# Four attention blocks forward and backward on one core: the queue of the last drain in a written order, and the weight-gradient operands in swapped buffers

## The chip, the cores and the metric

The kernel runs on one core of one Trainium2 chip. The core has a matrix engine (TensorE, PE in the profile; its weight loads are the rows PEld), a vector engine (VectorE, DVE), a scalar engine (ScalarE, ACT), a general engine (GpSimd, POOL) and a sync engine (SyncE, SP) that here only issues DMA transfers. The metric is the device time of one execution in microseconds (us); lower is better.

## The reference

Two kinds of block, A and B, follow each other as A, B, A, B on an input of 2048 rows by 640 columns, with 32 heads of width 20. The second A uses the weights of the first, and the second B those of the first B. The reference returns the output and the gradients of the input and of the four weight matrices.

```
def _A_ref(x, wqkv, wo):                 # linear attention
    q, k, v = split(x @ wqkv)
    phi = lambda t: where(t > 0, t + 1, exp(t)) + 1e-6
    pq, pk = phi(q), phi(k)
    kv, z = einsum("bhsd,bhse->bhde", pk, v), einsum("bhsd->bhd", pk)
    o = einsum("bhqd,bhde->bhqe", pq, kv) / (einsum("bhqd,bhd->bhq", pq, z) + 1e-6)
    return o @ wo
def _B_ref(x, wqkv, wo):                 # attention to the last 256 rows
    p = softmax(where(mask, q @ k.T * Dh ** -0.5, -1e9))
    return (p @ v) @ wo
x = A_x
x = x + _A_ref(_layernorm(x), A_wqkv, A_wo)
x = x + _B_ref(_layernorm(x), B_wqkv, B_wo)
x = x + _A_ref(_layernorm(x), A_wqkv, A_wo)
x = x + _B_ref(_layernorm(x), B_wqkv, B_wo)
out, vjp = jax.vjp(f, A_x, A_wqkv, A_wo, B_wqkv, B_wo); grads = vjp(grad_out)
```

All arrays are bfloat16. The blocks are called layers 0 to 3 below: 0 and 2 are A, 1 and 3 are B.

## The kernel before, in words

The rows are cut into 16 tiles of 128. `passes` is a generator that runs the whole program in stages: the forward pass of all layers, the backward core of layer 3, the backward pass of layer 2, the backward core of layer 1, and then, without a break, the last drain, the backward pass of layer 0 and the weight gradients. `run` asks for one stage after the other. For each it opens a block in which the order of the instructions on an engine is the order in which Python emits them. PE, DVE, ACT and POOL are always in that block. SP is in it only where the entry of `SPM` is true; elsewhere the framework's scheduler chooses the place of each DMA issue in SP's queue. SP works through its queue strictly in order: an issue that has to wait holds up every later one.

Two other devices set the order. `slots` spreads a list of small functions over numbered slots, by the offsets in the table `PLACES`. And where SP is in order, `put` doesn't issue a DMA at once: it stores it with a delay in slots from `PLACES["sp"]`, and `tick`, called once a slot, issues what is due.

**The core of a B layer** goes over eight chunks of two tiles. What follows a chunk (`plan_behind`) turns its gradient `dq` (128 x 2 x 1920) into `dqT`, multiplies with `WTB` into `dh`, closes the layer norm (`lna`, `gn`), turns `gn` (`gT`), multiplies with `WoTA` into `dn`, and adds an outer product of `dn` and `pqb` into `macc`. It loads `hnb`, `gc`, `oa` and `pqb`, and stores `dq`, `gn` and `dn`. For the last two chunks, 6 and 7, most of that happens after the core has ended.

**The last drain** is that rest for layer 1: a list `left1` of functions, one a slot. It is also where the weight gradients begin, since their matmuls need nothing from the drain. `weight_jobs` is a generator of them: a job is one block of columns of one weight matrix, five groups of 32 matmuls (128 x 160 for Wo of B, 128 x 240 for W of B, then wider ones for A). A group needs `lhs`, two halves of four DMAs each (640 KB a DMA), and `rhs`, four DMAs of 320 KB for Wo of B. Matmuls 0 to 15 of a group read the first half of `lhs`, 16 to 31 the second; each DMA feeds four of them. After a group, DVE or ACT copies the sum into `wr`, which has five buffers and is stored by one DMA. `fill(us)` takes matmuls from the generator up to a credit of so many us.

At slot 8 of the drain the generator is called for the first time, which issues all loads of the first job. From slot 25 on, each slot emits its own function and then `fill(1.0)`. After the drain `macc` is closed into `dmz` and turned.

**The backward pass of layer 0** follows with 16 tiles of eight slots each, with `fill(0.8)` a slot. A tile loads `ldn`, `lv`, `lpqk`, `lhn`, `lg` for two tiles at a time, turns three of them on PE (L205), forms `dqa`, turns it, multiplies with `WTA` and stores `dqa` to DRAM (`dqkv`). `dqa` has two buffers. When the last job of Wo of B ends, the second half of the next `lhs` is loaded into a buffer that this job has used. The generator then asks for 8.0 us of credit without any matmul, so ten slots pass that hold no weight-gradient matmul; this is called the gap below. When the layer is finished, the remaining weight gradients run alone.

**Buffers.** The first job's `lhs` halves (the stored `o` of layers 3 and 1) come from one pool `wl` of two buffers, first buffer first. The first of these lies where the last `dq` of the core was.

Lines: `put` L134, `tick` L142, the drain L1520 to L1561, the store of a weight-gradient block L1299. All DMA issues have line L129, nearly all matmuls L185 and the turns of PE L205, L1082, L1158 and L252.

Of the kernel before, what the change touches and what calls it, by code (L numbers as in the profile page):

```python
# [15 lines left out]
P = 128  # L16
# [5 lines left out]
TT = T // P  # L22
DT = D // P
SPM = (True, True, False, True, False)
G = H // 4
# [24 lines left out]
    sp=[4, 2.1, 1, 0.6, 2.6, -2.1, 0.5, 0.4, 2, 1.8, 1.1, 0.8, 3, 1, 0.9, 0.5, 1.3, 1.1, 1, 1],  # L50
# [3 lines left out]
    bl3=[13.4, 15, 15.5, 16.2, 17.3, 17.7, 18.5, 20.2, 25.9, 28.6, 29.3, 36, 19.7, 19.9, 20.3, 22.7, 23.9, 24.8, 26.3, 26.7, 30.1, 31.8, 33.1, 36.4, 40.2, 44.6, 13.4, -5.7, -4.4, 14, 19.4, 35.1],  # L54
    bl1=[13.4, 15, 15.8, 16.8, 17.4, 17.7, 19.7, 21.4, 26.1, 27.8, 30.5, 36, 19.2, 20, 20.3, 21.7, 23.7, 24.6, 25.1, 25.9, 29.6, 31.8, 32.8, 35.8, 40.1, 44.6, 0, -6, -5, -2, 0, 1],
    la=[-10.3, -2.5, 2.1, 2.4, 1.9, 3.2, 4.6, 6.2, 7.2, 8, 4.9, 8, 8.3, 10, 11.8, 13.9, 14, 16.2, 16.9, 17, 19.2, -2.3, 3.6],
# [13 lines left out]
    xx=[1, 0, 1, 1, 0, 0, 0, 0, 1, 0, 1, 0, 0, 0, 0, 0, 0, 1, 0, 0, 1, 0, 0, 1],  # L70
    bd=[0, 1, 0, 0, 0, 0, 0, 1, 0, 1, 1, 0, 1, 1, 0, 0, 0, 1, 1, 1, 0, 1, 0, 0])


class Kern:
# [58 lines left out]

    def put(self, kind, out, in_, transpose=False, now=False):  # L134

        d = PLACES["sp"][kind]
        if not self.spm or d <= 0 or now:
            self.dma(out, in_, transpose)
        else:
            self.queue.append((self.now + d, len(self.queue), out, in_, transpose))  # L140
# [804 lines left out]
    def plan_behind(self, st, l, c, dq, g_out):  # L945

        nc = self.nc
        la = l - 1
        x = {}
        r = self.r[la]  # L950
        last = c == TT // 2 - 1
        ex = last and l == 1

        def load():
# [3 lines left out]
        def turn(i):  # L958
            assert dq["n", c] == 8
            x["dT", i] = st.sp.tile([P, NF, P], BF, name="dqT", bufs=3)  # L960
            if c == TT // 2 - 2 or (c == TT // 2 - 1 and i == 0):
                self.turn_pe(st, x["dT", i], dq[c][:, i, :])
            else:
                self.put(7, x["dT", i], dq[c][:, i, :], transpose=True)

        def store():
            assert dq["n", c] == 8
            self.put(8, self.pair(self.dq[l], c), dq.pop(c))

# [6 lines left out]
        def store_g():  # L976
            assert x["gn", 0] and x["gn", 1]
            self.put(9, self.pair(g_out, c), x["gn"])

        def store_dn():  # L980
            assert x["rd", 0] is not None and x["rd", 1] is not None
            self.put(10, self.pair(self.sv[la]["dn"], c), x["dn"].rearrange("p b h d -> p b (h d)"))

# [235 lines left out]
    def weight_jobs(self, W):  # L1219
# [54 lines left out]
        while job is not None:  # L1274
# [6 lines left out]
            for m in range(DT):  # L1281
                if m == 1:
                    job = after(i0, c0, w)
                    if job is not None:
                        nxt = ls, rhs(mats[job[0]][1], job[1], job[2])
                if m == 2 and job is not None and job[1] == 0:
                    L2 = mats[job[0]][0]
                    nxt = [lhs(L2[0]), None if W.tight else lhs(L2[1])], nxt[1]
                ps = W.ps.tile([P, 512], F32, name="wg")
                for i in range(n):  # L1290
                    self.mm(ps[:, 0:w], ls[i // TT][:, i % TT, m * P:(m + 1) * P], r[:, i, 0:w], i == 0, i == n - 1)
                    if i < n - 1:
                        yield w / 2400.0
                o = W.out()
                if m % 2:
                    nc.scalar.copy(o[:, 0:w], ps[:, 0:w])  # L1296
                else:
                    nc.vector.tensor_copy(o[:, 0:w], ps[:, 0:w])  # L1298
                self.dma(out[m * P:(m + 1) * P, c0:c0 + w], o[:, 0:w])  # L1299
                yield w / 2400.0  # L1300
# [136 lines left out]
    def passes(self):  # L1437
# [6 lines left out]
        with ExitStack() as rest:  # L1444
# [80 lines left out]
            W.ps = self.pool(rest, "wp", 2, bass.MemoryType.PSUM, "right")  # L1525
            wl = self.pool(rest, "wl", 2)
            W.big, W.turn, W.wide, W.late = self.pool(rest, "wq", 1).tile([P, 2, 2 * TT, 240], BF, name="rhs"), 0, False, None
            wo = self.pool(rest, "wo", 5)
            st.ex = self.pool(psl, "ex", 1)
            W.lhs, W.tight = [wl, wl], True  # L1530
            W.out = lambda: wo.tile([P, 240], BF, name="wr")
# [10 lines left out]
            for j, f in enumerate(left1):  # L1542
                if f is not None:
                    f()
                if j == 8:
                    next(jobs)
                if j == 20:
                    self.fetch(WTA, self.WT["A"])
                if j > 24:
                    fill(1.0)  # L1550
            self.close_outer(self.dmz)
            self.turn_outer(st, self.dmz, self.dmzT)
            psl.close()
            es.close()

            with ExitStack() as es, ExitStack() as le:
# [15 lines left out]
            wl4 = self.pool(rest, "wl", 2)  # L1572
            W.lhs += [wl4, wl4, wl, wl3]
            W.tight, W.wide = False, True
# [70 lines left out]
```

## Time and profile before

| | |
|---|---|
| time, median of 3 runs | 2173.22 us (2174.26, 2164.63, 2173.22) |
| the profiled execution | 2163.42 us, span 2161.7 us |
| PE busy | 2021.7 us, 94% of the span |
| DVE / ACT / POOL busy | 65% / 61% / 48% |
| DMA on SP's queue | 674976 packets, 420.52 MB |

The span is the time from the first to the last instruction of the profiled execution, and its own time is 1.7 us longer. The profile gives, for each engine, the busy time in windows; for a group of instructions, its count, its mean duration and what ended the idle time before it; for SP, when each DMA was issued and how long until it landed; and a chain of waits followed back from the last instruction. A row of the timeline holds a start, a duration, and the number of instructions of one kind that followed each other without a break; the duration of a run of matmuls contains the passage of the last one through the array. In the profile the drain begins at about 1648 us, the first turn of layer 0's backward pass (`flip<-ident,ldn`) is at 1729.17 us, its last matmul is at 1945.8 us, and the rest is weight gradients.

### The profile page before, as it was taken

Reading aid. Unit: us, or ns where it says so; the run is one execution under the profiler, and the core shown is the slowest. Engines: PE = TensorE matmul, PEld = TensorE weight load, DVE = VectorE, ACT = ScalarE, POOL = GpSimd, SP = SyncE. Lnnn points to the kernel's source line nnn. Section 1 sums busy time; section 2 is a strip of 40 time slices with the busy share of each in tenths; the row PEclk is TensorE's granted clock in tenths of the full one; section 3 lists DMA queues with packets and bytes.
Section 4 is the critical chain, followed back from the end, with each engine's and each line's share of the span. In section 5 each row is a group of like instructions: output and inputs, shape, how many; then the busy total and the mean of one; then the engine's idle time right before and its main releaser. Section 6 shows DMA issues by size and latency. Waiting matters only on the chain.

```text
span 2161.7 us, 77047 instructions
## 1 busy us (share of the span) xinstructions
PE 2021.7 (94%) x32885; PEld 1563.7 (72%) x32885; DVE 1400.5 (65%) x2828; ACT 1314.6 (61%) x1866; POOL 1032.9 (48%) x1643
## 2 busy tenths in 40 slices
PE   8889998899987999999979999999998899999999
PEld 6667776677766877777758778777776788888644
DVE  7789996788844888888748678888885233320000
ACT  6568887478875787777647667777775143330000
POOL 1046666156666577777524566777764111220000
PEclk9999999999999999999999999999998999999999
DMA  7598886698874379898899724899987899978650
GB/s 250 198 233 209 213 213 168 199 226 217 216 200 139 92 157 191 188 191 179 182 283 274 199 75 122 185 188 188 191 182 194 264 306 229 285 193 263 204 164 21
DMA packets 675320, 425.45 MB, mean 197 GB/s; under 512 B 399264, under 2 KB 653984, under 8 KB 674592
## 3 DMA queue, kind: packets, MB, share of 16 engines
q1 hardware_dynamic: 674976, 420.52, 76.3%
q8 instruction: 257, 4.21, 0.8%
q14 instruction: 87, 0.71, 0.1%
HBM read 195.17 MB, written 144.70 MB: 157 GB/s over the span
## 4 chain that ended last, share of the span: by engine, by line
PE 49%; DVE 8%; POOL 7%; DMA 6%; ACT 5%; issue 4%; SPq 1%; DVEq 0%; POOLq 0%; ACTq 0%
PE dense L185 16%; PE wg L185 15%; DVE ds L790 5%; PE acc L185 4%; PE dp L185 3%; PE flip L205 3%; PE flip L812 2%; POOL e L805 2%; DMA pqb<-pqk 1%; ACT e L786 1%; PE sT L185 1%; PE ops L185 1%; PE flip L216 1%; POOL e L801 1%; SPq L129 1%
## 5 line engine op out<-in xcount | busy, mean ns | idle before, releaser
L790 DVE TENSOR_TENSOR ds<-dp,e 128x1024 bf16<-128x1024 f32 (+1 forms) x384 | 443.7, 1155 | 120.8 <-PE s L185 70.6
L786 ACT ACTIVATE e<-s 128x1024 bf16<-128x1024 f32 (+1 forms) x384 | 374.9, 976 | 113.0 <-PE s L185 91.4
L448 ACT ACTIVATE eT<-sT 128x2048 bf16<-128x2048 f32 x180 | 338.0, 1878 | 94.1 <-PE sT L185 64.7
L185 PE MATMUL wg<-rhs,lhs 128*128 128x240 bf16 (+3 forms) x2880 | 373.7, 286 | 9.7 <-DMA lhs<-o 9.7
L185 PEld LDWEIGHTS <-lhs 128*128 128x128 bf16 x2880 | 260.7, 98 | 99.4 <-DMA lhs<-o 12.5
L805 POOL TENSOR_SCALAR_AFFINE_SELECT e<-e 128x256 bf16<-128x256 bf16 x512 | 207.5, 421 | 164.4 <-ACT e L786 164.1
L185 PEld LDWEIGHTS <-dqT 128*128 128x128 bf16 x1920 | 174.4, 98 | 60.0 <-issue 4.4
L456 POOL TENSOR_SCALAR_AFFINE_SELECT eT<-eT 128x512 bf16<-128x512 bf16 x256 | 165.2, 649 | 104.5 <-ACT eT L448 101.3
L185 PE MATMUL acc<-slabqs,ds 128*128 128x20 bf16 x2880 | 195.6, 172 | 2.1 <-ACT dq L874 0.4
L185 PE MATMUL acc<-ds,e 128*128 128x20 bf16 x2880 | 193.3, 171 | 0.0
L185 PEld LDWEIGHTS <-ds 128*128 128x128 bf16 x2880 | 173.2, 96 | 19.7 <-issue 15.3
L185 PE MATMUL dp<-slabT,dT 32*128 32x128 bf16 (+1 forms) x1952 | 150.0, 244 | 29.4 <-DVE ds L790 23.4
L1298 DVE CAST wr<-wg 128x240 bf16<-128x240 f32 (+3 forms) x54 | 24.4, 452 | 233.0 <-PE wg L185 228.1
L801 POOL TENSOR_SCALAR_AFFINE_SELECT e<-e 128x512 bf16<-128x512 bf16 x224 | 142.5, 636 | 59.6 <-ACT e L786 55.1
L185 PEld LDWEIGHTS <-e 128*128 128x128 bf16 x2880 | 164.2, 96 | 5.0 <-issue 0.9
L1296 ACT CAST wr<-wg 128x240 bf16<-128x240 f32 (+3 forms) x36 | 14.3, 396 | 245.8 <-PE wg L185 233.2
L1190 POOL TENSOR_TENSOR dh<-dh,lg 128x640 f32<-128x640 f32 x32 | 46.1, 1440 | 242.7 <-DVE s L1187 240.2
L185 PE MATMUL dense<-WB,hnT 128*128 128x320 bf16 x960 | 160.0, 303 | 1.7 <-ACT hnT L208 0.7
L185 PE MATMUL dense<-WTA,dqT 128*128 128x320 bf16 x960 | 158.0, 301 | 0.6 <-DVE dqT L1161 0.3
L812 PE MATMUL flip<-ident,ds 128*128 128x128 bf16 x1920 | 152.9, 221 | 3.4 <-DVE ds L911 3.4
L185 PE MATMUL dense<-WTB,dqT 128*128 128x320 bf16 x960 | 153.8, 301 | 0.0
L185 PE MATMUL s<-slabT,slabqT 32*128 32x128 bf16 (+1 forms) x1952 | 147.0, 245 | 4.5 <-ACT e L786 4.5
(184 smaller groups left out, 4478.4 us busy)
## 6 DMA issues: line engine op xcount, KB each, us to landing
T<-T SPq DMA_DIRECT2D x96, 256.0 KB, 4.1
s<-s SPq DMA_DIRECT2D x32, 512.0 KB, 3.1
slabT<-T SPq DMA_DIRECT2D x64, 256.0 KB, 3.6
dqkv<-dq SPq DMA_DIRECT2D x16, 960.0 KB, 6.9
dqkv<-dqa SPq DMA_DIRECT2D x32, 480.0 KB, 4.3
rhs<-dqkv SPq DMA_DIRECT2D x32, 480.0 KB, 5.7
rhs<-dqkv SPq DMA_DIRECT2D x16, 960.0 KB, 7.7
hn<-hn SPq DMA_DIRECT2D x64, 160.0 KB, 3.5
```

The source lines that it names most:

```text
L129: return self.nc.sync.dma_start(out=out, in_=in_, transpose=transpose)
L185: return self.nc.tensor.matmul(out, lhsT=lhsT, rhs=rhs, start=start, stop=stop, skip_group_check=True, **kw)
L205: self.nc.tensor.transpose(t[0:w, j, :], src[:, c0:c0 + w], self.ident)
L448: nc.scalar.activation(e, s, ACT.Exp)
L456: nc.gpsimd.affine_select(out=e, in_=e, compare_op=ALU.is_ge, fill=0.0, base=0, pattern=[[0, 4], [1, P]], channel_multiplier=-1)
L786: nc.scalar.activation(u.e[:, :, 0:w], s[:, :, 0:w], ACT.Exp)
L790: nc.vector.tensor_tensor(out=d.ds[:, :, 0:w], in0=d.dp[:, :, 0:w], in1=d.e[:, :, 0:w], op=ALU.mult)
L801: nc.gpsimd.affine_select(out=v, in_=v, pattern=[[0, 4], [1 if far else -1, P]], **kw)
L805: nc.gpsimd.affine_select(out=v, in_=v, pattern=[[0, 2], [1 if far else -1, P]], **kw)
L812: nc.tensor.transpose(ps[:, 4 * j + i, :], f.ds[:, j, i * P:(i + 1) * P], self.ident)
L1190: nc.gpsimd.tensor_tensor(out=x["dh"], in0=x["dh"], in1=L["g"][:, i, :], op=ALU.add)
L1298: nc.vector.tensor_copy(o[:, 0:w], ps[:, 0:w])
```

## The change

Four things are changed. `SPM` gets a sixth entry and `passes` one more `yield`, so that the last drain is a stage of its own with SP in Python's order, and layer 0's backward pass starts a new stage in which the scheduler places the DMA issues as before. In the drain, DMAs that go through `put` get delays from the new table `sd` for the last two chunks: the `dq` store has none, the stores of `gn` and `dn` wait about three slots, the store of a weight-gradient block 3.5 slots (`dj`). The first job's loads are issued after slot 3 and not 8, and a slot's credit is 0.7 and not 1.0, so fewer weight-gradient matmuls stand in the drain and more behind it. The last chunk's offsets `bl1` are slightly different. And the two `lhs` buffers are two pools of one buffer, taken in the other order.

```diff
-SPM = (True, True, False, True, False)
+SPM = (True, True, False, True, True, False)
...
-    bl1=[13.4, 15, 15.8, 16.8, 17.4, 17.7, 19.7, 21.4, 26.1, 27.8, 30.5, 36, 19.2, 20, 20.3, 21.7, 23.7, 24.6, 25.1, 25.9, 29.6, 31.8, 32.8, 35.8, 40.1, 44.6, 0, -6, -5, -2, 0, 1],
+    bl1=[12.9, 15.1, 15.5, 16.2, 18.1, 19.6, 20.2, 22.2, 25.7, 27.8, 30.7, 34.2, 18.7, 19.4, 21.1, 21.6, 23.4, 24.3, 24.3, 25.9, 29.6, 31, 33.3, 35.3, 40.9, 45, 0.5, -4.8, -3.6, -1.2, 0.5, 1],
...
+    sd=[0.7, 0, 0, 3, 3, 3, 3, 3.9, 0, 0, 3.2, 2.6, 3.3, 3.1],
+    dj=[3, 21.9, 24, 3.5, 0.7, 8])
...
-    def put(self, kind, out, in_, transpose=False, now=False):
+    def put(self, kind, out, in_, transpose=False, now=False, delay=None):
-        d = PLACES["sp"][kind]
+        d = PLACES["sp"][kind] if delay is None else delay
...
+        tail = max(c - TT // 2 + 3, 0)
+        def wait(n):
+            return PLACES["sd"][n + 7 * (l == 1)] if tail else None
...
-                self.put(7, x["dT", i], dq[c][:, i, :], transpose=True)
+                self.put(7, x["dT", i], dq[c][:, i, :], transpose=True, delay=wait(0) if last else None)
...
-            self.put(8, self.pair(self.dq[l], c), dq.pop(c))
+            self.put(8, self.pair(self.dq[l], c), dq.pop(c), delay=wait(tail))
...
-            self.put(9, self.pair(g_out, c), x["gn"])
+            self.put(9, self.pair(g_out, c), x["gn"], delay=wait(2 * tail + 1))
...
-            self.put(10, self.pair(self.sv[la]["dn"], c), x["dn"].rearrange("p b h d -> p b (h d)"))
+            self.put(10, self.pair(self.sv[la]["dn"], c), x["dn"].rearrange("p b h d -> p b (h d)"), delay=wait(2 * tail + 2))
...
-                self.dma(out[m * P:(m + 1) * P, c0:c0 + w], o[:, 0:w])
+                self.put(0, out[m * P:(m + 1) * P, c0:c0 + w], o[:, 0:w], delay=PLACES["dj"][3])
...
-            wl = self.pool(rest, "wl", 2)
+            wl, wl2 = self.pool(rest, "wl", 1), self.pool(rest, "wl", 1)
...
-            W.lhs, W.tight = [wl, wl], True
+            W.lhs, W.tight = [wl2, wl], True
...
-                if j == 8:
+                if j == min(int(PLACES["dj"][0]), len(left1) - 2):
                     next(jobs)
-                if j == 20:
+                if j == min(int(PLACES["dj"][1]), len(left1) - 1):
                     self.fetch(WTA, self.WT["A"])
-                if j > 24:
-                    fill(1.0)
+                if j > PLACES["dj"][2]:
+                    fill(PLACES["dj"][4])
+                self.tick()
             self.close_outer(self.dmz)
             self.turn_outer(st, self.dmz, self.dmzT)
+            self.flush()
             psl.close()
             es.close()
+            yield
...
-            W.lhs += [wl4, wl4, wl, wl3]
+            W.lhs += [wl4, wl4, wl2, wl3]
```

What this makes of the order, engine by engine: up to the first transfers of the drain nothing moves. POOL's order is the same throughout, DVE and ACT exchange neighbours in the drain. On PE the same matmuls stand in another mixture: 236 weight-gradient matmuls ahead of the turn of `dmz` instead of 316, and 376 instead of 460 ahead of the first turn of `ldn`. The gap falls one tile later: before, it holds the turns of tile 2's and tile 3's `ldn`, after the change those of tile 3's and tile 4's. On SP the order in the drain is new, and behind it the scheduler puts the loads and stores of layer 0 and of the weight gradients in other places too:

```
before: hnb, gc, oa, pqb, rhs x4, dqT(chunk 7), dqkv(6), oa, pqb, dqkv(7), g, rhs, lhs x8, WTA, dn, wr1, rhs x3, wr2, g ...
after:  hnb, dqkv(6), oa, gc, oa, pqb(6), dqkv(7), dqT(7), pqb(7), rhs, lhs x2, rhs, lhs x2, rhs, lhs x2, rhs, lhs x2, g, WTA, rhs x4, dn, wr1, wr2, g ...
```

In the last part the eight `lhs` loads of Wo of A stand, before, one after the 56th and seven after the 57th stored block, with two `rhs` loads after the 55th. After the change one stands behind the 54th, two behind the 56th and five behind the 57th, and their `rhs` loads behind the 52nd to the 55th. That job starts when 60 blocks are done.

More of the change, by code (lines that the diff above doesn't have):

```diff
@@ L70 @@
     xx=[1, 0, 1, 1, 0, 0, 0, 0, 1, 0, 1, 0, 0, 0, 0, 0, 0, 1, 0, 0, 1, 0, 0, 1],
-    bd=[0, 1, 0, 0, 0, 0, 0, 1, 0, 1, 1, 0, 1, 1, 0, 0, 0, 1, 1, 1, 0, 1, 0, 0])
+    bd=[0, 1, 0, 0, 0, 0, 0, 1, 0, 1, 1, 0, 1, 1, 0, 0, 0, 1, 1, 1, 0, 1, 0, 0],
+    sd=[0.7, 0, 0, 3, 3, 3, 3, 3.9, 0, 0, 3.2, 2.6, 3.3, 3.1],
+    dj=[3, 21.9, 24, 3.5, 0.7, 8])
 class Kern:
```

## The prediction

> **What bounds the kernel now.** I read the page first, then the waits of PE from the drain on, then PE's and SP's timelines where those waits lie, and last the windows. From the page:
>
> ```profile
> span 2161.7 us, 77047 instructions
> PE 2021.7 (94%) x32885; PEld 1563.7 (72%) x32885; DVE 1400.5 (65%) x2828; ACT 1314.6 (61%) x1866; POOL 1032.9 (48%) x1643
> PE 49%; DVE 8%; POOL 7%; DMA 6%; ACT 5%; issue 4%; SPq 1%; DVEq 0%; POOLq 0%; ACTq 0%
> ```
>
> PE bounds it, and the change adds no matmul and removes none. It can move the time only through PE's idle time and through matmuls at the lower clock. SP's order differs from 1648 us on, PE's from about 1672. PE's waits from 1655 us to the end:
>
> ```profile
> PE wg L185 <- DMA lhs<-o: 9.7, 9, 1.7
> PE flip L1082 <- DVE dqa L1131: 4.1, 1, 4.1
> PE flip L205 <- POOL gn L1040: 1.9, 2, 1.2
> ```
>
> Columns are total us, times, longest. Some 16 us are in play. Six of the nine `lhs` waits lie in the drain; here they are in PE's timeline, with what follows:
>
> ```profile
> 1681.62 0.72 PE L185 MATMUL wg<-rhs,lhs 128*128 128x160 bf16 x8
> 1683.23 0.45 PE L185 MATMUL wg<-rhs,lhs 128*128 128x160 bf16 x4 [0.89 <-DMA lhs<-o]
> ...
> 1690.44 0.71 PE L185 MATMUL wg<-rhs,lhs 128*128 128x160 bf16 x4 [1.09 <-DMA lhs<-o]
> 1692.20 0.58 PE L185 MATMUL wg<-rhs,lhs 128*128 128x160 bf16 x3 [1.05 <-DMA lhs<-o]
> ...
> 1693.11 2.21 PE L185 MATMUL wg<-rhs,lhs 128*128 128x160 bf16 x15
> ...
> 1696.31 1.20 PE L185 MATMUL wg<-rhs,lhs 128*128 128x160 bf16 x15
> ```
>
> PE takes four matmuls from each `lhs` DMA as it lands. The six waits end 1.79 us apart, which for 0.655 MB is 366 GB/s. Fifteen matmuls then take 2.21 us, later 1.20. Why so late, in SP's timeline:
>
> ```profile
> 1649.95 1.43 SPq L129 DMA_DIRECT2D rhs<-in_grad_out_dram  x2
> 1651.42 4.21 SPq L129 DMA_DIRECT2D rhs<-g  x2
> 1661.56 1.66 SPq L129 DMA_TRANSPOSE dqT<-dq  x1
> ...
> 1666.54 0.58 SPq L129 DMA_DIRECT2D dqkv<-dq  x1
> ...
> 1673.80 9.31 SPq L129 DMA_DIRECT2D lhs<-o  x8
> 1683.15 2.27 SPq L129 DMA_DIRECT2D WTA<-WTAt  x1
> ```
>
> The first `lhs` DMA is issued 7.26 us after the second `dqkv` store. That store takes 6.5 us to land (median of two), and the first `lhs` buffer lies over the `dq` it reads. The windows (length, busy us of PE, PEld, DVE, ACT, POOL, clock, DMA share, GB/s):
>
> ```profile
> 1650.00:1660.00 10.00, 8.83 (x63) 7.12 (x63) 2.76 (x5) 2.53 (x5) 0.00 (x0) 0.57 0.94 249
> 1680.00:1690.00 10.00, 4.67 (x41) 3.09 (x39) 2.23 (x6) 2.39 (x5) 4.47 (x3) 0.80 1.08 374
> 1690.00:1700.00 10.00, 8.51 (x88) 7.70 (x89) 1.37 (x3) 1.68 (x3) 0.00 (x0) 0.69 0.97 346
> 1800.00:1850.00 50.00, 50.00 (x530) 44.37 (x528) 15.56 (x41) 18.18 (x38) 9.23 (x6) 1.00 1.09 252
> ```
>
> In the drain the transfers are at their rate and PE waits; from 1800 on PE never stops.
>
> **Step 1, the first job's loads.** In the new order SP issues `hnb` at 1647.95 as before, then the `dqkv` store of chunk 6, two `oa` and `gc`. `pqb` of chunk 6 has one buffer and must wait for PE's outer products of chunk 5, which end near 1656.0. Behind it wait the `dqkv` store of chunk 7, then `dqT`, which waits as before for its buffer until 1661.56. So SP frees the loads no earlier than 1661.56 + 1.66 = 1663.2; PE needs none of the held ones sooner. Then `pqb`, four `rhs` and eight `lhs` go out, two `lhs` to a `rhs`. `dqT` takes 4.1 us to land, 1665.7. At 249 GB/s, the window that holds the same `rhs` loads, 0.328 MB takes 1.3 us; an `lhs` takes 1.79. The last but one lands at 1665.7 + 5 x 1.3 + 7 x 1.79 = 1684.7, the last at 1686.5; before, 1690.4 and 1692.2.
>
> PE reaches these matmuls at 1681.62, by the same work as before. It does 11, the turn of `gn`, then 21. `gn` was ready at 1682.47 (POOL row 1680.93, 1.54 long); DVE now does one reduction of 0.48 us ahead of it, so about 1682.9, a wait of 0.5 that the later one swallows. Without waits the 32 would end at 1681.62 + 32 x 0.069 + 0.28 = 1684.1; with the last DMA at 1686.5 they end at 1686.8, so 2.7 us are lost. Before, 31 ended at 1692.57 against 1683.76, 8.8 lost, and the low clock behind them cost 0.30 + 1.01 + 0.53 = 1.8 (a turn 0.74 against 0.44, fifteen 2.21 against 1.20, five dense 1.37 against 0.84). I charge 1.0 for it now, for two waits and not six. Gain 10.6 - 3.7 = **6.9 us**. Bounds: all 6.88 MB at 249 GB/s would end at 1693.3, a loss of 1; at 374 GB/s at 1684.1, with no wait and a gain near 10. I take the middle, since `lhs` was carried at 366.
>
> [...]
>
> The rest of the drain follows PE. It holds 80 fewer weight-gradient matmuls up to `dmz`, and as many more later: 5.5 us moved, nothing saved. The longest chain it must still cover is chunk 7's second tile: dense, DVE 0.49, POOL 1.30 + 0.80, DVE 0.88 for two reductions, 3.5 us and some hand-over, against 74 matmuls x 0.069 = 5.1 us. The second job's four `rhs` land after `g` and `WTA`, about 1686.5 + 0.9 + 6.7 + 5.2 = 1699.3, and PE needs them at 160 matmuls, about 1699.9; that is close, and up to 1 us may be lost. The stores of `gn`, `dn` and `wr` go later; nothing of the drain reads the first two, and `wr` has five buffers. The `dq` stores, first in the queue, are read again only in the gap or later. `ldn` is issued behind the ninth `wr`, 52 matmuls (3.6 us) after `dmz` and 88 (6.1 us) before its turn; it landed 3 us after its issue. No cost.
>
> **Step 2, the gap.** Before, ten slots without weight-gradient matmuls ran from 1747.5 to 1764.57, 17.1 us for 9.7 us of work (45 `WTA` matmuls x 0.136, 24 + 15 turns x 0.056, small products). The 4.1 us wait lies in it: a `dqkv` store had been queued behind four `lhs` loads. Now that store is ahead of those loads, but the gap reaches tile 4, whose `ldn` is issued behind the four other `lhs` loads, and these may start only when the last job's matmuls end. With the gap's start as 0: issue at 0.9, first landing 4.6 later (the shortest of any `lhs`), three more x 1.79, then `ldn` 0.9: 11.8. PE has 8.2 us of work until then, so it waits 3.6, and loses about 3.0 to the low clock after, as it did before (3.1 us of work in 6.15). Gain 7.4 - 6.6 = **0.8 us**. Bounds: at 249 GB/s, 16 us, a loss of 4; were the wait gone, +7. I take the rate at which `lhs` was carried.
>
> **Step 3, the `lhs` of Wo of A.** Three waits, 2.9 us, at 1983 to 1988, and two runs of four matmuls that took 0.72 and 1.15 us against 0.54, 0.8 more. The eight loads stood one behind the 56th and seven behind the 57th block; now three are out before the 57th. A block is 32 x 0.1025 = 3.3 us, so two go 3.3 us earlier and need 3.6 us of the rate. The last would land 4.4 us earlier than 1987.9, when PE wants it at 1984.2. Gain **3.7 us**, bounds 0 (if the `rhs` loads, now beside them, take the time back) and 3.7.
>
> **Step 4**, the swap alone: the later loads have the same readers and orders. It acts through step 1, where it parts `lhs` from the `dq` store. The offsets only exchange neighbours. 0.
>
> Sum 6.9 + 0.8 + 3.7 = 11.4 us. Against the profiled execution's own 2163.42 (span 2161.7 and 1.7 around it) that is 2152.0. The four executions shown lie at two levels, 2163.4 and 2164.6, and 2173.2 and 2174.3; the median of runs is 2173.22, by which the sum is 2161.8. I forecast from the mean of the four, 2168.9: **2157.5 us**.
>
> **Rivals.** (a) The `lhs` loads are not what bounds the drain: PE then waits for `gn`, or for `rhs` at the low rate. For it: 1682.47 for `gn` is only just in time, and 249 GB/s in the window with `rhs`. Against: the waits of before name `lhs` alone. Step 1 gives 0 and the rest 4.5 at best: 2164 to 2169, middle 2166.
>
> (b) Slower: SP's written order. All twelve loads stand behind two waits of SP for PE, and the four `rhs`, which landed before 1660 in an idle stretch, now share the late one. If the 6.88 MB move at 150 GB/s they end at 1665.7 + 45.9 = 1711.6, 19.4 later than before; less 4.5 of steps 2 and 3, 2183.8. It takes over half a percent from 1707.5 on, that is below 165 GB/s. For it: the queue mixes four kinds of row; 204 GB/s stood from 1660 to 1670. Against: that window holds SP's pause, and 336 to 374 follow.
>
> (c) The wait in the gap disappears too, if `ldn` comes before PE: 11.4 + 6.6 = 18, 2150.9. Against: four loads stand ahead of it.
>
> **How the numbers follow.** Forecast (gains of 6 to 15) 0.48, (c) 0.07, (a) 0.28, (b) 0.17. I call half a percent, 10.8 us, about what a measurement can tell from no change. Faster by more: 0.45 of the forecast and (c), 0.52. Within: (a) and the rest, 0.31. Slower: (b), 0.17. The range runs from 2146, the forecast from the lower level with step 1 at its upper bound, 2163.4 - 10 - 0.8 - 3.7 = 2148.9 and the scatter below it, to 2174, the upper level with no gain.
>
> **What would show it.** Right: the first `lhs` issue near 1664, PE's `lhs` waits in the drain below 3 us in sum, the first `ldn` turn near 1716, a wait of 3 to 4 us at tile 4's `ldn` turn near 1755, no `lhs` wait near the end. Wrong: an `lhs` issue after 1670, a wait of PE for `rhs` or `gn`, SP held at `pqb` beyond 1657, or a wait in layer 0's steady part, which had none.

## The result and the profile after

The changed kernel takes 2160.19 us by the median of 14 runs (2153.57 to 2167.12), the kernel before 2166.32 by the median of 14 (2156.95 to 2174.26). The ratio is 0.9971, with a 95% interval of 0.9957 to 0.9985: 6.1 us, or 0.29%, faster, which is inside the half percent that I had called about what a measurement can tell. The forecast was 2157.5. A second comparison, told below, gave 0.9953 (0.9935 to 0.9971).

The page of the changed kernel, in the lines that answer to those of before:

```profile
span 2160.0 us, 77067 instructions
PE 2019.3 (93%) x32885; PEld 1563.7 (72%) x32885; DVE 1400.4 (65%) x2828; ACT 1314.5 (61%) x1866; POOL 1031.8 (48%) x1643
PE 50%; DVE 7%; DMA 6%; POOL 5%; ACT 5%; issue 4%; SPq 2%; DVEq 0%; POOLq 0%; ACTq 0%
```

The spans differ by only 1.7 us, because the changed kernel's profiled execution was already 7.7 us later when it came to the drain: SP issued the last `hnb` at 1655.62 us and not at 1647.95, although the program is the same up to there. I therefore count from that issue, called H. The profiles show how large the scatter ahead of H is: over all fourteen it lies between 1645.0 and 1655.6.

PE's waits from 1655 us to the end (total us, times, longest):

```profile
PE flip L207 <- DMA ldn<-dn: 5.3, 1, 5.3
PE wg L187 <- DMA lhs<-o: 3.7, 3, 2.5
PE flip L207 <- POOL gn L1046: 2.2, 3, 1.2
PE dense L187 <- DMA dqT<-dqa: 1.9, 1, 1.9
```

The nine `lhs` waits of 9.7 us have become three of 3.7. The 4.1 us wait for `dqa` in the gap has gone, and one of 5.3 for tile 4's `ldn` stands there. The wait for `dqT` is new. In PE's timeline:

```profile
1686.10 0.93 PE L187 MATMUL wg<-rhs,lhs 128*128 128x160 bf16 x11
1687.48 0.45 PE L207 MATMUL flip<-ident,gn 128*128 128x128 bf16 x5 [0.46 <-POOL gn L1046]
1687.77 1.06 PE L187 MATMUL wg<-rhs,lhs 128*128 128x160 bf16 x13
1691.36 0.71 PE L187 MATMUL wg<-rhs,lhs 128*128 128x160 bf16 x4 [2.52 <-DMA lhs<-o]
1693.04 0.71 PE L187 MATMUL wg<-rhs,lhs 128*128 128x160 bf16 x4 [0.96 <-DMA lhs<-o]
1693.54 1.54 PE L187 MATMUL dense<-WoTA,gT 128*128 128x320 bf16 x5
1694.88 1.67 PE L187 MATMUL wg<-rhs,lhs 128*128 128x160 bf16 x11
...
1767.97 0.90 PE L207 MATMUL flip<-ident,ldn 128*126 128x128 bf16 x6 [5.27 <-DMA ldn<-dn]
...
1797.17 0.85 PE L187 MATMUL dense<-WTA,dqT 128*128 128x320 bf16 x5 [1.87 <-DMA dqT<-dqa]
```

Twenty-four of the first 32 matmuls run without a wait; the last eight wait 3.48 us for the last two `lhs` DMAs, and what follows runs at half speed (five dense products in 1.54 us, 0.84 a little later). The window from 1690 to 1700 has a granted clock of 0.66. Later the `lhs` of Wo of A costs PE one wait of 0.17 us, where it was 2.9.

SP's timeline in the drain:

```profile
1655.62 0.55 SPq L131 DMA_DIRECT2D hnb<-hn  x1
1656.43 0.36 SPq L131 DMA_DIRECT2D dqkv<-dq  x1
...
1661.96 0.36 SPq L131 DMA_DIRECT2D pqb<-pqk  x1
1662.37 0.46 SPq L131 DMA_DIRECT2D dqkv<-dq  x1
1666.11 1.65 SPq L131 DMA_TRANSPOSE dqT<-dq  x1
1667.80 1.34 SPq L131 DMA_DIRECT2D pqb<-pqk  x1
1669.49 0.38 SPq L131 DMA_DIRECT2D rhs<-in_grad_out_dram  x1
1669.92 1.12 SPq L131 DMA_DIRECT2D lhs<-o  x2
```

SP is held for `pqb` and for `dqT` as foreseen, and the first `lhs` goes out 14.3 us behind H, where before it was 25.8.

Windows of 5 us, from 5 us behind H on, show the other side of it (the last three columns are the granted clock, the DMA share and GB/s):

```profile
1660.62:1665.62 5.00, 4.65 (x42) 3.49 (x42) 1.18 (x2) 1.38 (x3) 0.00 (x0) 1.00 1.02 356
1665.62:1670.62 5.00, 4.49 (x34) 3.02 (x31) 0.96 (x3) 2.52 (x7) 2.28 (x2) 1.00 1.03 251
1670.62:1675.62 5.00, 2.96 (x19) 1.68 (x20) 1.45 (x4) 1.66 (x4) 3.58 (x3) 0.77 0.99 307
1675.62:1680.62 5.00, 5.00 (x37) 3.54 (x36) 1.08 (x3) 1.31 (x3) 2.09 (x2) 0.89 1.11 341
```

The DMA engines are full also while SP is held, for `pqb` up to 1661.96 us and for `dqT` up to 1666.11: the share is 1.02 and 1.03 in the first two windows.

All profiles of this study, in us behind H: when PE starts the first weight-gradient matmul, when the last of the first job's eight `lhs` DMAs lands, and when the program ends; then the time from that first matmul to the end. The total of matmuls between those two points is the same in all of them.

| kernel | first wg matmul | last lhs | end | first wg to end |
|---|---|---|---|---|
| before | 33.7 | 44.2 | 513.8 | 480.1 |
| before, second profile | 32.3 | 42.3 | 512.2 | 480.0 |
| before, third profile | 29.8 | 40.5 | 509.9 | 480.1 |
| changed | 30.5 | 37.4 | 504.4 | 473.9 |
| changed, second profile | 30.3 | 36.9 | 503.9 | 473.7 |
| swap alone | 30.8 | 37.4 | 507.7 | 476.9 |
| order without swap | 30.4 | 37.0 | 503.9 | 473.6 |
| changed, credit 1.0 | 29.8 | 37.0 | 507.6 | 477.8 |
| changed, one store twice | 30.8 | 39.8 | 506.2 | 475.4 |
| changed, loads split | 29.8 | 37.5 | 503.7 | 473.9 |
| split, tile 4 earlier | 30.2 | 37.9 | 495.3 | 465.1 |
| the same, rhs from ScalarE | 34.5 | 37.2 | 493.0 | 458.5 |
| the same, loads at slot 1 | 29.8 | 36.1 | 495.1 | 465.4 |
| the same, two groups interleaved | 29.8 | 37.2 | 490.0 | 460.2 |

The last column repeats within 0.2 us for the two kernels that were profiled more than once, where the executions behind the medians differ by over 10 us. In part that is luck. In the three profiles of before the pieces of it scatter more and cancel: the drain by 1.9 us, the gap by 1.6, the last thousand weight-gradient matmuls by 1.4. So with one profile each, a difference of 1 or 2 us in this column has to be borne out by the waits that make it. By it the change is worth 480.04 - 473.76 = 6.3 us.

### The profile page after: what moved, and what is told of

It reads as the page before. It is cut to its first block, busy times and chain, and to the rows that moved or that the text cites. A ratio compares the mean times of both kernels' runs of the same rounds, so it can differ in the third digit from the quotient of the medians.

```text
span 2160.0 us, 77067 instructions
## 1 busy us (share of the span) xinstructions
PE 2019.3 (93%) x32885; PEld 1563.7 (72%) x32885; DVE 1400.4 (65%) x2828; ACT 1314.5 (61%) x1866; POOL 1031.8 (48%) x1643
## 4 chain that ended last, share of the span: by engine, by line
PE 50%; DVE 7%; DMA 6%; POOL 5%; ACT 5%; issue 4%; SPq 2%; DVEq 0%; POOLq 0%; ACTq 0%
PE dense L187 17%; PE wg L187 15%; DVE ds L792 5%; PE acc L187 4%; PE dp L187 3%; PE flip L207 3%; PE flip L814 2%; DMA pqb<-pqk 2%; SPq L131 2%; PE flip L218 1%; ACT e L788 1%; POOL e L807 1%; PE ops L187 1%; PE sT L187 1%; DMA dsT<-ds 1%
```

## The experiments

My theory after the result was this: the drain gains about 4 us because the first job's loads no longer stand behind the store of `dq`; the end gains 3.6 us because the scheduler puts the `lhs` of Wo of A earlier; the gap gains nothing; and the new wait for `dqT` takes 1.9 back. Rivals: the swap alone makes the drain's gain; the order alone makes it; the credit has no part; all of it is scatter ahead of the change.

### The swap alone

```diff
-            wl = self.pool(rest, "wl", 2)
+            wl, wl2 = self.pool(rest, "wl", 1), self.pool(rest, "wl", 1)
-            W.lhs, W.tight = [wl, wl], True
+            W.lhs, W.tight = [wl2, wl], True
-            W.lhs += [wl4, wl4, wl, wl3]
+            W.lhs += [wl4, wl4, wl2, wl3]
```

> Theory A (the drain's gain comes from the first lhs loads no longer waiting for the dq store that they lay over; the written order itself costs some of it, since SP then puts all twelve loads behind pqb's and dqT's waits): before with the two lhs buffers swapped and nothing else starts its first two lhs loads right behind pqb near 1656.5 us and the other six near 1665; they land by about 1680, PE has no lhs wait left in the drain (8.8 us before) and the low clock behind it (1.8) goes too: 8 to 10 us less than before, 2157 to 2159 against 2166 medians, more than the whole change gave (6.2). The 4.1 us wait for dqa in the gap and the 2.9 us of lhs waits near 1985 stay. Rival B (the written order makes the gain, the swap nothing): within 1.5 us of before. Rival C (the difference of the two kernels lies in the stages that they share): within 1.5 us of before.

Measured: 2159.48 us against 2162.79, ratio 0.9986 (0.9968 to 1.0004), unclear by itself; from the first weight-gradient matmul to the end 476.9 us, 3.1 less than before. I had expected 8 to 10. SP's timeline says why:

```profile
1649.20 2.99 SPq L129 DMA_DIRECT2D lhs<-o  x2
...
1663.11 0.64 SPq L129 DMA_DIRECT2D dqkv<-dq  x1
1663.79 1.92 SPq L129 DMA_DIRECT2D lhs<-o  x2
1665.76 1.93 SPq L129 DMA_DIRECT2D rhs<-g  x1
1670.58 1.95 SPq L129 DMA_DIRECT2D lhs<-o  x2
```

The first half of `lhs` is free at once. But the second half now lies over that `dq`: its first DMA is issued at 1670.58, and the `dqkv` store issued at 1663.11 landed at 1670.51. The swap moves the wait from the first half to the second. PE still waits 4.2 us for `lhs` in the drain, 4.0 for `dqa` in the gap and 3.3 for the `lhs` of Wo of A.

### The order without the swap

```diff
-            W.lhs, W.tight = [wl2, wl], True
+            W.lhs, W.tight = [wl, wl2], True
```

> The whole change with the lhs buffers in their old order. Theory A, in its strong form (the first half waits for the store of the last dq wherever it stands): the store is issued near 1662.4 us and takes 6.5 us, the turned load of the same dq lands near 1670.2, and the first lhs was issued at 1669.9 with the swap: it now goes out less than 1 us later. So the order alone keeps 5 to 6 of the 6.2 us, about 0.9973 of before, with lhs waits in the drain of 3.5 to 4.5 us. Theory A', the swap is needed beside the order: the first half starts behind the store's landing with 2 us or more, and only step 3's 3.6 us less the 1.9 of dqT remain: 2 us less than before or none.

Measured: 2152.00 us against 2162.79, ratio 0.9959 (0.9942 to 0.9976); 473.6 us in the last column, as the changed kernel. SP waited 1.1 us for the turned load of `dq` to land ahead of the first `lhs`, and that was all. So with the store ahead of the loads the swap is worth nothing, and the two do not add: either one alone brings the last `lhs` to 37.0 to 37.4 us. This run keeps everything else of the change; SP's order in itself, the delays of `sd` and the loads at slot 3 and not 8 were not taken apart.

### The credit as before

```diff
-    dj=[3, 21.9, 24, 3.5, 0.7, 8])
+    dj=[3, 21.9, 24, 3.5, 1.0, 8])
```

> The whole change with a slot's credit in the drain at 1.0 as before, not 0.7. Theory A: the gap falls back by a tile, the lhs loads of Wo of A stand again one behind the 56th and seven behind the 57th block, so the 2.9 us of waits near 1985 and the 0.8 behind them return (3.6 us lost); the dqT transposes stand ahead of lhn again, so that wait of 1.9 us is gone; in the drain PE reaches the last lhs loads about 1 us earlier and waits 1 us longer. Sum 6.2 - 3.6 + 1.9 - 1 = 3.5 us less than before (1 to 5). Rival B (the order in the drain is all of it, the credit nothing): 6 us less, as the whole change.

Measured: 2163.79 us against 2162.79, ratio 1.0000 (0.9985 to 1.0015), and 477.8 us in the last column: 4.0 worse than the changed kernel, and 2.3 better than before, where I had expected 3.5. Its `lhs` waits are 4.1 us in the drain and 3.3 at the `lhs` of Wo of A, which stands again one behind the 56th and seven behind the 57th block; its two waits for `ldn` are 6.2 us; the wait for `dqT` is gone. The gap holds the turns of tile 2's and tile 3's `ldn` again, as before. The credit, 0.7 and not 1.0, is what makes step 3, and it comes with the gap one tile on and another choice of the scheduler.

### Both kernels again

> The kernel before, profiled a second time, to see how much of a profile is scatter. Theory S (the stretch ahead of the first weight-gradient matmul is scatter of the granted clock): from the issue of the last hnb to that matmul it takes 30 to 31 us and not 33.7, so that the end lies 510 to 511 us behind that issue; the stage of the change, from that matmul on, again takes 480 us, with lhs waits of 9 to 10 us, a dqa wait of 4 us in the gap. Rival (the 33.7 us belong to the kernel before, since its dq store and dqT stand later): 33 to 34 us again.

> The changed kernel once more, beside the others on the same chip. Both theories: about 2160 us by the median, 0.997 of before; from the issue of the last hnb to the end 503.5 to 505.5 us, with the same three waits: lhs in the drain 3.5 us, ldn in the gap 4.5 to 5.5, dqT behind lhn 1.9.

Measured: the kernel before 480.0 us in the last column; 32.3 us to the first matmul, so the question of that stretch stayed open. The changed kernel 2154.58 us by the median of 10 against 2164.02, ratio 0.9953 (0.9935 to 0.9971), with waits of 3.5 for `lhs`, 5.4 for `ldn` and 2.2 for `dqT`.

> The kernel before, profiled a third time. From the issue of the last hnb to the first weight-gradient matmul it took 33.7 and 32.3 us, and in the eleven other profiles, those of the changed kernel and of the experiments whose ScalarE issues nothing, 29.8 to 30.8. If that is scatter of the granted clock, a third profile has a good chance to lie below 31; if it belongs to the kernel before, it lies at 32 to 34 again, with turns and dense products at half clock between 17 and 25 us behind hnb. From the first weight-gradient matmul to the end 479.5 to 480.5 us by both.

(The profiles meant there are ten, not eleven.) The third profile of before has 29.8 us. The first shows, ahead of the change's first effect:

```profile
1655.90 9.65 PE L185 MATMUL dense<-WTB,dqT 128*128 128x320 bf16 x60
...
1668.70 1.37 PE L185 MATMUL dense<-WTB,dqT 128*128 128x320 bf16 x5
```

and the third:

```profile
1655.90 8.31 PE L185 MATMUL dense<-WTB,dqT 128*128 128x320 bf16 x60
...
1667.36 0.84 PE L185 MATMUL dense<-WTB,dqT 128*128 128x320 bf16 x5
```

The same instructions, 1.34 and 0.53 us longer. From H to the first weight-gradient matmul the granted clock was 0.79 in the first profile, 0.88 in the second and 1.00 in the third. That stretch is scatter of the granted clock, and the profile that I predicted from was the slow one: 3.9 us later at the first weight-gradient matmul than the third. Whether the old order makes a low clock there likelier stays open: that way takes 32 us and more in two of the four profiles with it, and in none of the nine with the new order in which ScalarE issues no loads.

### One store twice

```diff
-            self.put(8, self.pair(self.dq[l], c), dq.pop(c), delay=wait(tail))
+            d = dq.pop(c)
+            for _ in range(2 if l == 1 and c == TT // 2 - 2 else 1):
+                self.put(8, self.pair(self.dq[l], c), d, delay=wait(tail))
```

> The changed kernel, with the dq store of chunk 6 issued twice in the drain (the same 0.98 MB to the same place). Read from the issue of the last hnb, which leaves the scatter ahead of it out: the changed kernel lands its last lhs 37.1 us behind that issue and loses 3.6 us to lhs waits. Theory R (from that issue to the last lhs the transfers are at their rate all the time, so the order among them no longer matters and the bytes alone set the last landing): the extra store takes about 2.8 us at 350 GB/s, the last lhs lands at 39.5 to 40.5 us, PE waits 6 to 6.5 us, and from the first weight-gradient matmul to the end it takes 3 us more than the 473.8 of the changed kernel. Rival H (SP's two holds, for pqb and for dqT, set the start of the lhs loads, and the queue is empty beside them): the store hides in the hold, the last lhs lands at 37 to 38 us, nothing moves by more than 1 us.

Measured, one profile: the last `lhs` lands at 39.8 us behind H and not at 36.9 or 37.4, as the transfers' rate would have it. PE's waits for `lhs` in the drain are 5.3 us in sum, the longest 2.81, against 3.5; the last column is 1.6 higher, half of the 3 that I expected. But the edit adds a hold of SP as well as bytes. SP's timeline:

```profile
1649.15 0.36 SPq L131 DMA_DIRECT2D dqkv<-dq  x1
...
1650.07 1.02 SPq L131 DMA_DIRECT2D oa<-o  x1
1654.81 0.36 SPq L131 DMA_DIRECT2D dqkv<-dq  x1
...
1665.26 1.13 SPq L131 DMA_DIRECT2D lhs<-o  x2
```

The second store writes to the same place as the first. It goes out at 1654.81 us, just after the first has landed at 1654.79. The first `lhs` then leaves 16.9 us behind H and not 14.1 or 14.3: `pqb` goes out 1.1 us later than in the changed kernel, and SP's row of `dqT` takes 4.25 us and not 1.65; why it does so isn't shown. So this run by itself doesn't tell theory R from rival H. What speaks for R is the DMA share: 0.99 while SP stood at the second store (1651.09 to 1654.81), and from H to the last `lhs` 1.05 at 328 GB/s, as in the changed kernel (1.05 at 326). The engines had work all through the holds. And in the run with ScalarE's queue below, the last `lhs` is issued 3.7 us earlier and lands no earlier. I therefore read that the transfers between H and the last `lhs`, and not their order or SP's holds, now set when that DMA lands; it is argued from the share, and no run adds bytes without a hold. The table agrees: in all rows but this one and those of the kernel before it lands at 36.1 to 37.9 us, in several orders.

### The loads of layer 0 split

```diff
-        return ([(a[0], load)] if i == 0 else []) + list(zip(a[1:], fs))
+        loads = [(a[0], load)]
+        if l == 0 and t > 2:
+            loads = [(a[0], lambda: load(0)), (a[0] + 7, lambda: load(1))]
+        return (loads if i == 0 else []) + list(zip(a[1:], fs))
```

(`load(0)` issues `ldn`, `lv` and `lpqk`, `load(1)` the other two.)

> The changed kernel with lhn and lg of a pair seven slots later from tile 4 on, and nothing else: PE's wait for dqT in layer 0 (1.9 to 2.2 us) should go, the one for ldn in the gap (5.4) stay. From the first weight-gradient matmul to the end 471.5 to 472.2 us against 473.8. Rival: lhn was not what held the dqT transposes, the wait stays and the stretch takes 473.5 to 474.

Measured, one profile: no wait for `dqT`, so `lhn` had held the transposes. In the changed kernel SP stood at `lhn` from 1785.86 to 1790.93 us, and the next transposes were issued at 1792.37:

```profile
1785.44 0.42 SPq L131 DMA_DIRECT2D lpqk<-pqk  x1
1790.93 0.36 SPq L131 DMA_DIRECT2D lhn<-hn  x1
...
1792.37 3.57 SPq L131 DMA_TRANSPOSE dqT<-dqa  x2
```

The last column did not fall all the same (473.9): here the drain was 1.5 to 2.1 us longer than in the two profiles of the changed kernel, with 4.4 us of `lhs` waits and not 3.5, because the first matmul came at 29.8 us and the last `lhs` no earlier. From the turn of `dmz` on it is 1.5 to 1.9 us shorter.

### The loads of layer 0 split, tile 4's earlier

```diff
+            loads = [(a[0] - (5 if t == 4 else 0), lambda: load(0)), (a[0] + 7, lambda: load(1))]
```

> The whole change, and in layer 0 from tile 4 on a pair's loads are split: ldn, lv and lpqk stay at their slot, lhn and lg come seven slots later, where their buffers are free; and tile 4's ldn, lv and lpqk come five slots earlier, ahead of the four lhs loads of the gap. Theory A: the 5.3 us wait for ldn goes with about 2 us of low clock behind it, and the 1.9 us wait for dqT behind lhn goes: 8 to 9 us less than the changed kernel, about 15 less than before (0.993). Rival D (next in line in the gap is the store of dqa behind the same four lhs loads, as in the kernel before, where PE waited 4.1 us for it): PE waits 3 to 5 us for dqa instead, and only the 1.9 us of dqT and 1 or 2 us more are gained: 2 to 4 us less than the changed kernel, 0.996.

Measured: 2147.64 us against 2162.79, ratio 0.9932 (0.9909 to 0.9955), and 465.1 us in the last column, 8.7 below the changed kernel. The waits of PE that are left from 1655 us to the end, in its first two lines:

```profile
PE wg L187 <- DMA lhs<-o: 4.6, 4, 2.5
PE flip L207 <- POOL gn L1046: 1.7, 2, 1.2
```

No wait for `ldn`, none for `dqa`, none for `dqT`. The theory's numbers hold, and the store of `dqa` was not next in line. The gap's loss lay in the order on SP, `ldn` behind the four `lhs` loads, and could be had back in full.

### rhs from ScalarE's queue, beside the last edit

```diff
-                    self.dma(r[:, i * TT + a:i * TT + a + 8, 0:w], R[i][...])
+                    nc.scalar.dma_start(out=r[:, i * TT + a:i * TT + a + 8, 0:w], in_=R[i][...])
```

> As the kernel with the split and earlier loads, and the first job's four rhs loads are issued from ScalarE's queue, not SP's. Theory A (twelve loads in one row behind pqb and dqT are what the drain waits for): the rhs loads leave the row and move while SP is held; 4 x 1.2 us fewer stand between the lhs loads, the last lhs lands about 33 us behind the issue of hnb and not 37.9, PE's lhs waits in the drain fall from 4.4 us to 1 or less with the low clock behind them: 4 to 6 us less than that kernel, 0.991 of before. Rival F (ScalarE sits on the chain of the drain, and four issues of about 1 us on it delay dqT's copies and dh, so PE waits there): no gain, or up to 3 us more than that kernel.

Measured: 2148.93 us against 2164.02, ratio 0.9925 (0.9898 to 0.9953), by the medians no better than without it. ScalarE's rows:

```profile
1664.75 0.89 ACTq L1268 DMA_DIRECT2D rhs<-in_grad_out_dram  x1
1665.68 4.26 ACTq L1268 DMA_DIRECT2D rhs<-g  x2
1670.04 0.53 ACT L1018 ACTIVATE dh<-dense,rs 128x320 f32<-128x320 f32 x1 [5.31 <-issue]
```

The issues held `dh` for over 4 us, and PE then waited 5.05 us for `gn` and started the weight gradients at 34.5 us. The last `lhs` was issued 25.6 us behind H and not 29.4, and landed at 37.2, not at 33 as my theory had it. So Theory A was wrong: the loads came no earlier, and PE had no `lhs` wait because it was itself late. The rival's mechanism came, but without a loss: in the one profile of each, this kernel ends 2.3 us earlier behind H (493.0 against 495.3). The last column, which starts with PE's late arrival, overstates that. The transfers set the landing here too.

### The loads at slot 1, beside the same edit

```diff
-    dj=[3, 21.9, 24, 3.5, 0.7, 8])
+    dj=[1, 21.9, 24, 3.5, 0.7, 8])
```

> As the kernel with the split and earlier loads, and the first job's loads are issued after slot 1 of the drain and not 3, which puts them ahead of the last pqb, still behind dqT. Theory A: all twelve loads start 1.7 us earlier, the lhs waits in the drain fall from 4.4 to about 2.7 us: about 2 us less than that kernel. Rival G (the last pqb now comes behind twelve loads, lands near 39 us behind hnb's issue, and the last outer products wait for it): no gain or 1 to 3 us more.

Measured: 2143.77 us against 2164.02, ratio 0.9908 (0.9881 to 0.9936), but 465.4 us in the last column, no gain over the kernel without it. The last `lhs` lands at 36.1, 1.8 earlier, and PE's waits for `lhs` fall from 4.6 to 3.5 us; small new waits behind the drain (0.6 for a later `lhs`, 0.3 for `lpqk`, 0.3 for `dnT`) stand against that. No wait for `pqb` came. What its median has over the other's isn't in this column; it is within the two intervals.

### Two groups interleaved, beside the same edit

```diff
-            for m in range(DT):
+            for ms in [[0, 1], [2], [3], [4]] if (i0, c0) == (0, 0) else [[m] for m in range(DT)]:
...
-                ps = W.ps.tile([P, 512], F32, name="wg")
+                pss = [W.ps.tile([P, 512], F32, name="wg") for _ in ms]
                 for i in range(n):
-                    self.mm(ps[:, 0:w], ls[i // TT][:, i % TT, m * P:(m + 1) * P], r[:, i, 0:w], i == 0, i == n - 1)
+                    for ps, m in zip(pss, ms):
+                        self.mm(ps[:, 0:w], ls[i // TT][:, i % TT, m * P:(m + 1) * P], r[:, i, 0:w], i == 0, i == n - 1)
```

> The kernel with split and earlier loads, and the first job's first two groups are interleaved: each lhs DMA that lands feeds four matmuls of both (eight in all), so that the last landing leaves 8 matmuls behind it and 56 are done before, not 4 and 28. Theory R (the last lhs landing is fixed by the bytes): PE has 2.2 us more work to do under the same wait, so the wait falls from 4.4 to about 2.5 us and the low clock behind it shrinks: 2 to 3 us less than that kernel from the first weight-gradient matmul on (465.1 there), about 0.992 of before. Rival: PE waits for each landing as before, and the sums' copies now come in twos, so a later group waits for its PSUM buffer: no gain, or 1 us more.

Measured: 2142.63 us against 2164.38, ratio 0.9908 (0.9890 to 0.9927), and 460.2 us in the last column, 4.8 below the kernel without it, about twice what I expected. PE's timeline:

```profile
1684.20 0.52 PE L187 MATMUL wg<-rhs,lhs 128*128 128x160 bf16 x5 [0.40 <-DMA lhs<-o]
...
1685.88 0.73 PE L187 MATMUL wg<-rhs,lhs 128*128 128x160 bf16 x8 [0.68 <-DMA lhs<-o]
1686.45 0.84 PE L187 MATMUL dense<-WoTA,gT 128*128 128x320 bf16 x5
1687.13 0.85 PE L187 MATMUL wg<-rhs,lhs 128*128 128x160 bf16 x10
```

The last `lhs` lands when it did, at 37.2 us, but PE fills the time with the second group: waits of 1.1 us and not 4.4 us, and behind them no row at half speed (dense 0.84, ten matmuls 0.85). That is 3.3 us less waiting, and I put the other 1.5 down to the clock: in the drain of the kernel without it the granted clock was one half for 3.41 us, here never. This version is faster than both kernels: its interval lies below that of the changed kernel (0.9935 to 0.9971). Most of that comes from the split and earlier loads, which it contains.

## Why the prediction was right or wrong

**The size.** The sum said 11.4 us, the last column 6.3, the medians 6.1. The time was in the range, 2.7 us above the forecast, and the mechanisms are those named, but only 0.29% came out where I gave 0.52 to more than half a percent. Rivals (a) and (b) fell: PE's `gn` wait in that place was 0.46 us, it waited for no `rhs`, and the last `lhs` landed 3.1 to 6.8 us earlier behind H, not 19 later. (c) fell: the gap kept its loss. That the time came so near the forecast is partly luck: I had started from 2168.9, which is 2.6 above the 2166.32 that the kernel before takes by the median of 14, and the gain fell 5.3 short. Of the signs, the first `lhs` issue, the wait at tile 4's `ldn` and the vanished waits near the end came. The `lhs` waits in the drain were 3.48 us and not below 3. Four `lhs` issues came after 22 us behind H, the 1670 of the sign of being wrong, though SP waited for nothing there: each took it 1.6 to 1.7 us while the DMA engines were full (a share of 1.10 to 1.11 from 1675.62 to 1690.62).

**Step 1 was mis-sized: 6.9 predicted, 4.1 measured.** The measure is the time from the first weight-gradient matmul to the turn of `dmz`, less 0.0688 us for each weight-gradient matmul in it (316 before, 236 after; in unbroken rows at full clock one starts 0.069 us after the other): 15.2, 14.1 and 16.0 us before, 11.3 and 10.7 after; the means differ by 4.1. The new queue went as told: the first `lhs` 14.3 us behind H (1664 less 1647.95 would be 16), the last landing at 37.4 (38.5 forecast), the first turn of `ldn` at 68.1 behind H, which is the 1716 of the forecast to 0.1 us. That last agreement is luck: PE came 3.2 us sooner and lost as much more on the way. What failed is the line "PE reaches these matmuls at 1681.62, by the same work as before". It is the same work, but in that profile it ran at a low clock, as the third profile showed; in most other profiles PE is there 29.8 to 30.8 us behind H and not 33.7. In the kernel before that matters little, since its `lhs` loads hang on PE's progress and come earlier too (40.5 in the third profile). In the changed one they don't: they come when the bytes have passed, PE arrives 3 us sooner and waits it out. The first 32 matmuls take 7.7 us there (7.1 in the second profile), 5.2 and 4.6 more than their work by the prediction's own count, where it had 2.7. The second miss is the charge for the low clock, 1.0, where the rows after the waits are 1.9 us too long in sum (dense 1.54 against 0.84, eleven matmuls 1.67 against 0.92, an outer product 0.84 against 0.49, ten 0.97 against 0.85).

That charge was my estimate, by the number of waits: two and not six. Behind the two, of 2.52 and 0.96 us, the granted clock was 0.66 from 1690 to 1700 us, where with the six it had been 0.80 and 0.69 (1680 to 1690 and 1690 to 1700 us); with two of 0.40 and 0.68 us in the interleaved kernel no row ran at half speed.

**Step 2, the gap: 0.8 predicted, a loss of about 1.0 measured.** The place was right, a wait at tile 4's `ldn`; it was 5.27 us and not 3.6. The issue came 1.0 us after the gap's start (0.9 forecast), but the first `lhs` took 6.2 us to land and not 4.6, the shortest that I had found, and `ldn` landed at 13.5 and not 11.8. With 2.3 us of low clock behind it (the next four rows of PE against their length elsewhere) the gap loses 7.6 us, and 7.8 in the second profile. Before, it was 7.4 in the profile that I predicted from, but less in the other two: between the same two matmuls PE took 17.38, 16.88 and 15.82 us there, which makes losses of 7.4, 6.9 and 5.8. Their waits are 4.11, 3.68 and 3.71 us, and the granted clock was one half for 6.83, 6.83 and 3.41 us. In the first profile:

```profile
1757.61:1764.42 6.81, 6.00 (x34) 4.01 (x35) 2.90 (x7) 1.74 (x4) 0.00 (x0) 0.50 1.06 373
```

and in the third:

```profile
1757.04:1760.45 3.41, 3.30 (x24) 2.59 (x24) 1.96 (x6) 1.43 (x4) 0.00 (x0) 0.50 1.07 362
1760.46:1763.80 3.34, 3.34 (x37) 2.75 (x36) 0.17 (x2) 1.05 (x3) 0.00 (x0) 1.00 1.06 396
```

**A wait that I had not seen: -2.0** (1.87 and 2.18 in the two profiles). I listed a wait in layer 0's steady part as a sign of being wrong, and it came: `dqT` behind `lhn` in SP's row. I had compared which loads and stores the scheduler puts between which blocks, but had not asked of each whether SP would be held at it, and what stands behind it. The split shows the cause.

**Step 3 was right in what it named, and too small: 3.7 predicted, 5.2 measured.** Waits of 2.9 to 3.3 us went down to 0.17 and none, and the kernel with credit 1.0 shows that they come back with the old places. From the start of the last thousand weight-gradient matmuls to the end, with the same matmuls in both kernels, it takes 185.6, 187.0 and 186.3 us before and 181.2 and 181.0 after. So besides the waits 1.6 to 3.0 us were lost there, and not the 0.8 that I had read from two rows; the granted clock was one half for 3.41, 6.83 and 3.41 us. (The prediction's "from 1800 on PE never stops" holds for the window that it was read from, which ends at 1850.)

**Step 4, the swap, was right at 0 on top of the order**, but not for the reason given: I let it act "through step 1". The rest of the change alone does all of step 1, and the swap alone, which I had not priced, does three quarters of it.

Summed, 4.1 - 1.0 - 2.0 + 5.2 = 6.3, the 6.3 of the last column. These are means over three profiles of before and two of after. Each piece scatters by 1.4 to 1.9 us in those of before, so the split is sure to about 1 us.

## What to carry to other kernels

Before a wait in a profile is priced, profile the same kernel twice more: a stretch at low clock moved PE's arrival by 3.9 us here, and it is the arrival that says how long a transfer is waited for. Once the reordered queue had filled the DMA engines in this drain (a share of 1.05 from H to the last `lhs`), further reordering there brought little: the last `lhs` landed at 36.1 to 37.9 us in every kernel but the one before (40.5 to 44.2) and the one with the store twice (39.8). What helped was to give PE more work for each DMA that lands, as the two interleaved groups did. And when a scheduler puts loads in other places, look in the new order for each issue that can be held and for what then stands behind it.

## What was not expected of the hardware

- The same instructions behind the same waits of PE (1.22, 0.79 us) ran at half speed in two of three profiles of one program and at full speed in the third: the five dense products that follow took 1.37 and 1.33 us, and 0.84. With an earlier stretch of low clock in the first profile, the way from H to the first weight-gradient matmul took 29.8 to 33.7 us.
- The granted clock is one half or full in these traces, and a value between is a mean. Behind H the kernel before shows stretches at one half of 3.41, 10.24, 6.83 and 3.41 us in its first profile, and the changed kernel 3.41, 6.83 and 6.83 (apart from the last of each, in which the program ends). Waits of much the same length cost PE different times: 3.68 and 3.71 us in the gap of before, with losses of 6.9 and 5.8.
- Four DMA issues on ScalarE's queue took it 5.6 us (0.43, 0.89 and 4.26 for two) while SP's queue was busy, where SP's own issues of the same loads took 0.4 to 1.8 us each; the computing instruction behind them on ScalarE, `dh`, started after 5.31 us without one.
- A 0.98 MB store put into a stretch in which SP stood still for most of the time was not hidden: the last load behind it landed 2.5 to 2.9 us later. SP stood for 3.7 us at it, with a DMA share of 0.99.
